# Load order, place of attention 1, norm chain of group 0 and g_norm load in a fused linear-attention and ELU-MLP kernel

## The chip, the cores and the metric

The kernel runs on one NeuronCore of a Trainium2 chip. The metric is the device time of the slowest core in microseconds; there is only one core here. Times below are medians of several runs, always compared with runs of the kernel before on the same chip, interleaved with them. A kernel's profile is one further look at one execution; its span is about 2 us shorter than the time of that same run (328.3 against 330.45 us for the kernel before).

Engines in the profile: PE is TensorE (matrix products), PEld its weight loads, DVE is VectorE, ACT is ScalarE, POOL is GpSimd, SP is SyncE, which here issues the loads and stores.

## The reference, cut to what matters

```python
# q, k, v: (8, 8, 576, 64) float32; g_norm: (64,)
kv  = einsum('bhsd,bhse->bhde', k, v)
out = einsum('bhsd,bhde->bhse', q, kv)
rms = sqrt(mean(out * out, -1) + 1e-6)
x   = (out / rms * g_norm)  ->  (4608, 512)          # 4608 tokens
h   = x @ w_in                                       # w_in  (512, 2048)
g   = where(h > 0, h, exp(min(h, 0)) - 1)            # ELU
y   = g @ w_out                                      # w_out (2048, 512)
```

The kernel works in nine groups of 512 tokens: one for each batch entry, and one for the 64 tokens that each entry has left. A group goes through attention, the first product (`mm1`, eight steps of 8 matmuls with the ELU behind each), and the second product (`mm2`, four row blocks of 16 matmuls).

## The kernel before

All compute is in program order on each engine; an engine that waits holds up everything behind it: in the profile before, TensorE is idle for 2.07 us ahead of 90.92 us, waiting for `xT` of group 2, and the second-product matmuls of group 1 that stand behind those products come at 94.58, though the DVE steps they read had ended by 90.20. These are the parts that matter.

```python
g_src = bass.AP(tensor=g_norm.tensor, offset=g_norm.offset, ap=[[1, 64], [1, 1]])
for i in range(2):
    nc.scalar.dma_start(out=g_col[i * 64 : i * 64 + 64, :], in_=g_src)   # 64 x 4 bytes, issued by ACT
...
def mm1(T, i, cols=..., relu=False):
    h_ps = ps_m1.tile([P, 2, G], FP32, tag="mm1")      # two such PSUM buffers in all
    ...                                                # 8 matmuls 128x512
    nc.scalar.activation(e, h_ps, AF.Exp)              # ACT
    ...                                                # relu=True: ACT also copies max(h, 0) out
    def rest():                                        # DVE: elu_e, then gT (reads h_ps if relu=False)
...
# group 0, norm: norm_a = square (ACT) + sum (DVE); norm_b = ln, exp (ACT) + scale (DVE)
norm_a(0); norm_a(1); norm_b(0); norm_a(2); turn(0); norm_b(1); norm_a(3)
turn(1); norm_b(2); turn(2); norm_b(3); turn(3)        # turn = 4 transposes (PE) + copy with g_col
...
at = attention(1)
for i in range(8):
    mm1(0, i, cols, relu=(i % 2 == 1))()
    if i == 5:
        at["q"]()
at["kv"]()
for s, n in enumerate(("se0", "se1", None, "x")):      # attention 1, covered by half of mm2(0)
    for j in range(2):
        mm2(0, j, 4 * s, 4 * s + 4)
    if n:
        at[n]()

at = attention(2)
steps = {1: "q", 2: "kv", 3: "se0", 5: "se1", 7: "x"}
for i in range(8):                                     # the loop of group 1
    rest = mm1(1, i)
    if i < 7:
        mm2(0, 2 + i // 4, 4 * (i % 4), 4 * (i % 4) + 4)
    rest()
    if i in steps:
        at[steps[i]]()
mm2(0, 3, 12, 16)
# then the loops of groups 2 to 8, all alike
```

`attention(T)` gives five steps: "q" transposes q (copied out by DVE, then ACT), "kv" forms the 64x64 products, "se0" and "se1" each apply them to half of the rows and normalize (square on ACT, sum on DVE, ln/exp on ACT, scale on DVE), "x" transposes the result into `xT`, which the next loop's `mm1` reads. All five share one PSUM tile, `at`.

TensorE's idle stretches in the start are partly filled with `idle(n)`, matmuls of zeros that nobody reads.

Of the kernel before, what the change touches and what calls it, by code (L numbers as in the profile page):

```python
# [8 lines left out]
FP32 = mybir.dt.float32  # L9
# [3 lines left out]
AX = mybir.AxisListType  # L13
# [3 lines left out]
def kernel(  # L17
# [43 lines left out]
    ctx.enter_context(tc.manual_schedule())  # L61

    g_col = const.tile([P, 1], FP32, name="g_col")
    g_src = bass.AP(tensor=g_norm.tensor, offset=g_norm.offset, ap=[[1, 64], [1, 1]])
    for i in range(2):
        nc.scalar.dma_start(out=g_col[i * 64 : i * 64 + 64, :], in_=g_src)
    eps_col = const.tile([P, 1], FP32, name="eps_col")
    nc.vector.memset(eps_col, 1e-6)
    bd_kv = const.tile([P, B, NPAIR, P], BF16, name="bd_kv")
# [41 lines left out]
    def fetch(b):  # L111
        fetch_q(b)
        for name, src in (("k", k), ("v", v)):
            out_, in_ = fetch_kv(name, src, b)
            nc.sync.dma_start(out=out_, in_=in_)

    def fetch_w_in(s):
        st = stage_tile()[:, 0:2048]
        nc.sync.dma_start(
            out=st.rearrange("p (c f) -> p c f", c=KC),  # L120
            in_=moe_w_in.rearrange("(c p) f -> p c f", p=P)[:, :, s * 512 : s * 512 + 512],
        )
        raw["wi", s] = st

    def fetch_w_out(s):
        st = stage_tile()[:, 0:2048]
        nc.sync.dma_start(
            out=st.rearrange("p (c f) -> p c f", c=KC),
            in_=moe_w_out.rearrange("(c p) f -> p c f", p=P)[:, 4 * s : 4 * s + 4, :],
        )  # L130
        raw["wo", s] = st
# [18 lines left out]
    def cast_q(b, eng):  # L150
        sv = q_tile(b)
        for j in range(J):
            copy_on(eng, bf["q", b][:, j], sv[:, j])

    def cast_kv(name, b, eng):
        sv = kv_tile(name, b)
        for lo, hi in ((0, 2), (2, 4), (4, 6), (6, 8), (8, 9)):
            copy_on(eng, bf[name, b][:, lo:hi], sv[:, lo:hi])

    def cast_w_in(s, eng):  # L160
        st = raw.pop(("wi", s)).rearrange("p (c f) -> p c f", c=KC)
        for c in range(KC):
            copy_on(eng, w_in_sb[:, c, s * 512 : s * 512 + 512], st[:, c, :])

    def cast_w_out(s, eng):
        st = raw.pop(("wo", s)).rearrange("p (c f) -> p c f", c=KC)
        for c in range(KC):
            copy_on(eng, w_out_sb[:, 4 * s + c, :], st[:, c, :])
# [50 lines left out]
                    )  # L219

    def square(se_ps, n):
        sq = attp.tile([P, 2, DM], BF16, name="sq", tag="sq")[:, 0:n, :]
        nc.scalar.activation(sq, se_ps, AF.Square)  # L223
        return sq

    def sum_heads(sq, n):
        ss = attp.tile([P, 2 * H], FP32, name="ss", tag="ss")[:, 0 : n * H]
        nc.vector.reduce_sum(  # L228
            out=ss, in_=sq.rearrange("p c (h e) -> p (c h) e", h=H), axis=AX.X
        )  # L230
        return ss

    def inv_rms(ss):
        nc.scalar.activation(ss, ss, AF.Ln, bias=eps_col, scale=1.0 / D)  # L234
        nc.scalar.activation(ss, ss, AF.Exp, scale=-0.5)  # L235

    def scale_rows(xs, se_ps, ss, n):
        nc.vector.tensor_tensor(  # L238
            out=xs.rearrange("p c (h e) -> p (c h) e", h=H),
            in0=se_ps.rearrange("p c (h e) -> p (c h) e", h=H),  # L240
            in1=ss.to_broadcast([P, n * H, D]),
            op=ALU.mult,
        )

    def attention(T):
        st = {}

        def kv():
            if T == B:
                return  # L250
            kv_ps = at_tile(FP32)
            for u in range(2):
                kv_mm(T, [kv_ps[:, 0:512], kv_ps[:, 512:1024]], u)
            kv_v = kv_ps.rearrange("p (s x e) -> p s x e", s=2, e=P)[:, :, 0:2, :]
            bd_v = bd_kv[:, T].rearrange("p (s u) e -> p s u e", s=2)
            for l in range(2):
                ls = slice(l * 64, l * 64 + 64)
                nc.scalar.copy(bd_v[ls, :, :, ls], kv_v[ls, :, :, ls])

        def q_t():  # L260
            qt_ps = at_tile(BF16).rearrange("p (r t) -> p r t", r=NPAIR)
            for p in range(NPAIR):
                q_t_mm(bf["q", T], qt_ps, p)
            qT = attp.tile([P, NPAIR, G], BF16, name="qT", tag="qT")
            st["qT"] = qT
            nc.vector.tensor_copy(out=qT[:, 0:2, :], in_=qt_ps[:, 0:2, :])  # L266
            nc.scalar.copy(qT[:, 2:4, :], qt_ps[:, 2:4, :])  # L267

        def se(h):
            def run():  # L270
                se_ps = at_tile(FP32).rearrange("p (c f) -> p c f", c=2)
                for c in range(2):
                    se_mm(T, 2 * h + c, st["qT"], se_ps[:, c, :])
                ss = sum_heads(square(se_ps, 2), 2)
                inv_rms(ss)
                if h == 0:
                    st["xs"] = attp.tile([P, J, DM], BF16, name="xs", tag="xs")
                scale_rows(st["xs"][:, 2 * h : 2 * h + 2, :], se_ps, ss, 2)

            return run  # L280

        def x_t():
            xs = st["xs"]
            xt_ps = at_tile(BF16).rearrange("p (r t) -> p r t", r=NPAIR)
            for c in range(KC):
                for j in range(J):
                    nc.tensor.transpose(  # L287
                        xt_ps[:, c, j * P : j * P + P],
                        xs[:, j, c * P : c * P + P],
                        ident,  # L290
                    )
            x = attp.tile([P, KC, G], BF16, name="xT", tag="xT")
            xT[T] = x
            nc.vector.tensor_scalar(  # L294
                out=x[:, 0:2, :], in0=xt_ps[:, 0:2, :], scalar1=g_col, scalar2=None, op0=ALU.mult
            )
            nc.scalar.mul(x[:, 2:4, :], xt_ps[:, 2:4, :], g_col)  # L297

        return {"kv": kv, "q": q_t, "se0": se(0), "se1": se(1), "x": x_t}
# [61 lines left out]
    def mm2_half(T, i):  # L361
        mm2(T, i // 2, 8 * (i % 2), 8 * (i % 2) + 8)
# [25 lines left out]
    for u in range(2):  # L388
        for out_, in_ in halves:
            nc.sync.dma_start(  # L390
                out=out_[:, 2 * u : 2 * u + 2, :], in_=in_[:, 2 * u : 2 * u + 2, :]
            )
    for s in range(3):
        fetch_w_in(s)

    q_st = q_tile(0)
# [5 lines left out]
    def idle(n):  # L402
        for _ in range(n):
            nc.tensor.matmul(idle_ps[:, 0, :], lhsT=ident, rhs=zeros, start=True, stop=True)  # L404
# [3 lines left out]
    for s in range(2):  # L408
# [2 lines left out]
        for p in (2 * s, 2 * s + 1):  # L411
            q_t_mm(bf["q", 0], qt_ps, p)
        idle(2)
    fetch_w_in(3)
    kv_st = [kv_tile(name, 0) for name in "kv"]
    kv_ps = [ps_m2.tile([P, DM], FP32, name="kv_ps", tag="mm2") for _ in range(2)]
    for u in range(2):
# [35 lines left out]
    one = [t.rearrange("p (c f) -> p c f", c=1) for t in se_ps]  # L453
    ss = {}

    def norm_a(j):
        ss[j] = sum_heads(square(one[j], 1), 1)

    def norm_b(j):
        inv_rms(ss[j])  # L460
        scale_rows(xs0[:, j : j + 1, :], one[j], ss[j], 1)

    def turn(j):
        js = slice(j * P, j * P + P)
        xt = xt_ps[:, j % 2, j // 2]
        for c in range(KC):
            nc.tensor.transpose(xt[:, c, :], xs0[:, j, c * P : c * P + P], ident)
        if j % 2 == 0:
            nc.scalar.mul(x0[:, :, js], xt, g_col)
        else:  # L470
            nc.vector.tensor_scalar(
                out=x0[:, :, js], in0=xt, scalar1=g_col, scalar2=None, op0=ALU.mult
            )
            idle(2)

    norm_a(0)
    norm_a(1)
    norm_b(0)
    norm_a(2)
    turn(0)  # L480
    norm_b(1)
    norm_a(3)
    turn(1)
    norm_b(2)
    turn(2)
    norm_b(3)
    turn(3)


    for s in range(4):  # L490
        cast_w_in(s, Q)
    fetch(1)
    cast_q(1, Q)
    cast_kv("k", 1, Q)
    cast_kv("v", 1, Q)
    for s in range(4):
        fetch_w_out(s)
    for s in range(4):
        cast_w_out(s, Q)

    def cast_all(b):
        cast_q(b, Q)
        if b < B:
            cast_kv("k", b, Q)
            cast_kv("v", b, Q)

    fetch(2)
    cast_all(2)
    at = attention(1)
    for i in range(8):  # L510
        cols = (slice(0, 256), slice(256, 512)) if i == 0 else (slice(0, 512),)
        mm1(0, i, cols, relu=(i % 2 == 1))()
        if i == 5:
            at["q"]()
    at["kv"]()
    for s, n in enumerate(("se0", "se1", None, "x")):
        for j in range(2):
            mm2(0, j, 4 * s, 4 * s + 4)
        if n:
            at[n]()  # L520

    at = attention(2)
    steps = {1: "q", 2: "kv", 3: "se0", 5: "se1", 7: "x"}
    fetch(3)
    for i in range(8):
        rest = mm1(1, i)
        if i < 7:
            mm2(0, 2 + i // 4, 4 * (i % 4), 4 * (i % 4) + 4)
        rest()
        if i in steps:  # L530
            at[steps[i]]()
    mm2(0, 3, 12, 16)

    steps = {0: "kv", 1: "q", 2: "se0", 4: "se1", 6: "x"}
    for T in range(2, NT):
# [45 lines left out]
```

## Time and profile before

| | before |
|---|---|
| median (4 runs of its first comparison) | 331.76 us (330.75 to 332.81) |
| first square of group 0 / first product of group 0 | 15.93 / 26.56 us |
| DVE's copy of `xT` of group 1 / of group 2 starts | 60.93 / 90.12 us |
| last unbroken run of second-product matmuls (71 of them) starts / span | 307.26 / 328.3 us |

The lines below are from the profile page of the kernel before: the busy time, and TensorE's busy tenths and granted clock in 40 equal slices of 8.2 us.

```profile
PE 299.2 (91%) x1903; PEld 151.0 (46%) x1939; DVE 180.3 (55%) x216; ACT 152.1 (46%) x216; POOL 78.5 (24%) x140
...
PE   8648796799789999999999999999999999999993
...
PEclk9996999999979999999999999999999999999999
```

TensorE is busy 91% of the span, and the slices that fall short lie in the first 98 us, but for the last one. The clock shows a dip to 0.6 in the fourth slice (from 24.6 us) and one to 0.7 in the twelfth (from 90.3 us).

The next view is busy time by stretch of the same run, with the granted clock, the DMA share (packet times over the time of 16 engines; it can come out a little above 1, here up to 1.07) and GB/s as the last three columns.

```profile
core 0: us, PE busy (x) PEld busy (x) DVE busy (x) ACT busy (x) POOL busy (x), PEclk, DMA share, GB/s
5.00:7.00 2.00, 2.00 (x8) 0.80 (x7) 0.43 (x1) 0.78 (x2) 0.00 (x0) 1.00 0.55 163
19.00:26.50 7.50, 2.68 (x16) 1.27 (x17) 3.88 (x7) 3.05 (x9) 5.71 (x11) 0.78 1.07 373
26.50:31.90 5.40, 5.30 (x25) 3.13 (x24) 0.68 (x1) 1.03 (x2) 4.01 (x8) 0.68 1.06 390
33.50:47.20 13.70, 11.53 (x64) 5.48 (x67) 8.18 (x11) 7.68 (x9) 13.70 (x22) 1.00 1.06 378
47.20:61.70 14.50, 10.39 (x100) 5.96 (x101) 8.89 (x9) 7.10 (x13) 8.38 (x16) 1.00 0.46 170
87.00:90.90 3.90, 1.85 (x20) 1.22 (x20) 3.65 (x5) 0.83 (x2) 0.00 (x0) 1.00 0.00 0
90.90:97.00 6.10, 5.53 (x34) 2.23 (x35) 1.02 (x2) 2.61 (x3) 0.00 (x0) 0.72 0.60 191
150.00:300.00 150.00, 149.05 (x938) 75.23 (x955) 90.26 (x104) 72.56 (x97) 18.13 (x32) 1.00 0.25 88
```

From 150 to 300 us TensorE is busy in 149.05 of 150 us: there it is the limit, and the change leaves that part alone. The time to win is earlier: 2.68 of 7.5 us busy in the norm of group 0, 11.53 of 13.7 in its first product, 10.39 of 14.5 where attention 1 stands alone, and 1.85 of 3.9 at the end of the loop of group 1. Three stretches have a low clock (0.78, 0.68 and 0.72).

The timeline of TensorE in the same run (start, duration, instruction group, and in brackets the idle time before it and what the profile says ended it):

```profile
26.56 5.29 PE L313 MATMUL h_ps<-xT,w_in_sb 128*128 128x256 bf16 x24
33.45 3.61 PE L313 MATMUL h_ps<-xT,w_in_sb 128*128 128x512 bf16 x15 [1.60 <-DVE gT L331]
38.54 3.61 PE L313 MATMUL h_ps<-xT,w_in_sb 128*128 128x512 bf16 x16 [1.47 <-POOL w_out_sb L137]
...
43.64 3.61 PE L313 MATMUL h_ps<-xT,w_in_sb 128*128 128x512 bf16 x15 [0.59 <-DVE gT L331]
...
90.92 0.59 PE L313 MATMUL h_ps<-xT,w_in_sb 128*128 128x512 bf16 x2 [2.07 <-DVE xT L294]
```

In the first product TensorE starts anew at 33.45, 38.54 and 43.64, that is every 5.1 us for two steps whose matmuls take 3.6 us: step i+2 needs the PSUM buffer that DVE's `gT` of step i still reads. The idle time at 38.54 is put down to a POOL cast of w_out, which that product doesn't read; what ended it is DVE's `gT`, which ended at 37.26 + 1.22 = 38.48 us. DVE's timeline in the same run:

```profile
37.26 1.22 DVE L331 TENSOR_TENSOR gT<-elu_e,h_ps 128x1024 bf16<-128x1024 bf16 x1
```

The first 24 products, 128x256 each, take 5.29 us, or 220 ns each. At 90.92 TensorE has been idle 2.07 us for `xT`.

### The profile page before, as it was taken

The numbers are of one execution on the slowest core, as the hardware profiler recorded it, in microseconds if no ns is written. First come the engines' busy times: TensorE is split into PE (matmuls) and PEld (weight loads), VectorE is DVE, ScalarE is ACT, GpSimd is POOL, SyncE is SP. The second block draws the span as 40 slices with busy tenths as digits, with TensorE's granted clock in tenths as the row PEclk, the third lists the DMA queues.
The fourth block names the chain that finished last, engine by engine and source line by source line (L and its number), as shares of the span: only waits on it lengthen the run. The fifth ranks groups of instructions, "written<-read, shape, count | busy, mean of one in ns | idle before, by whom it ended". The sixth has DMA issues, their size and how long they took to land.

```text
span 328.3 us, 4746 instructions
## 1 busy us (share of the span) xinstructions
PE 299.2 (91%) x1903; PEld 151.0 (46%) x1939; DVE 180.3 (55%) x216; ACT 152.1 (46%) x216; POOL 78.5 (24%) x140
## 2 busy tenths in 40 slices
PE   8648796799789999999999999999999999999993
PEld 3414353354335454545454554455445545444441
DVE  3462566367824774676467646755675577445400
ACT  3552574446345544555455445543654454433320
POOL 0077998063007200630070017001100000000000
PEclk9996999999979999999999999999999999999999
DMA  6999994670067106710851094114301010101122
GB/s 207 394 381 381 387 374 149 189 293 0 2 206 275 64 0 194 288 66 0 272 209 64 3 319 163 64 43 104 85 29 64 2 64 0 66 0 64 66 61 67
DMA packets 28565, 46.44 MB, mean 141 GB/s; under 512 B 5504, under 2 KB 13696, under 8 KB 28544
## 3 DMA queue, kind: packets, MB, share of 16 engines
q1 hardware_dynamic: 28384, 46.14, 39.8%
q8 instruction: 15, 0.25, 0.3%
q14 instruction: 6, 0.05, 0.0%
q10 hardware_dynamic: 160, 0.00, 0.0%
HBM read 36.70 MB, written 9.44 MB: 141 GB/s over the span
## 4 chain that ended last, share of the span: by engine, by line
PE 76%; DVE 7%; DMA 7%; ACT 4%; POOL 2%; issue 2%; SPq 1%; DVEq 0%
PE o_ps L347 34%; PE h_ps L313 33%; DMA st<-in_k_dram 4%; DMA st<-in_v_dram 3%; PE at L182 2%; DVE gT L331 2%; PE at L287 2%; PE at L204 2%; DVE ss L228 2%; DVE xs L238 2%; PE at L192 2%; POOL v_bf L137 1%; DVE elu_e L328 1%; ACT elu_e L321 1%; POOL k_bf L137 1%
## 5 line engine op out<-in xcount | busy, mean ns | idle before, releaser
L313 PE MATMUL h_ps<-xT,w_in_sb 128*128 128x512 bf16 (+1 forms) x565 | 136.3, 383 | 9.6 <-DVE xT L294 2.9
L347 PE MATMUL o_ps<-w_out_sb,gT 128*128 128x512 bf16 x561 | 134.4, 379 | 0.8
L321 ACT ACTIVATE elu_e<-h_ps 128x1024 bf16<-128x1024 f32 x72 | 73.4, 1021 | 57.0 <-PE h_ps L313 55.5
L313 PEld LDWEIGHTS <-w_in_sb 128*128 128x128 bf16 x584 | 56.5, 100 | 71.4 <-issue 10.3
L347 PEld LDWEIGHTS <-gT 128*128 128x128 bf16 x576 | 56.3, 98 | 67.5 <-issue 0.8
L331 DVE TENSOR_TENSOR gT<-elu_e,h_ps 128x1024 bf16<-128x1024 bf16 x68 | 83.0, 1221 | 7.1
L328 DVE TENSOR_SCALAR elu_e<-elu_e 128x1024 bf16<-128x1024 bf16 x72 | 34.0, 473 | 91.1 <-ACT elu_e L321 91.1
L137 POOL CAST q_bf<-st 128x512 bf16<-128x512 f32 x32 | 19.2, 637 | 131.8 <-DMA st<-in_q_dram 108.7
L357 ACT COPY o_sb<-o_ps 128x512 f32<-128x512 f32 x36 | 21.0, 583 | 21.8 <-PE o_ps L347 21.7
L238 DVE TENSOR_TENSOR xs<-at,ss 128x1024 bf16<-128x1024 f32 (+1 forms) x18 | 21.0, 1166 | 10.8 <-ACT ss L235 10.8
L228 DVE TENSOR_REDUCE ss<-sq 128x16 f32<-128x1024 bf16 (+1 forms) x20 | 22.2, 1112 | 8.2 <-ACT sq L223 8.0
L223 ACT ACTIVATE sq<-at 128x1024 bf16<-128x1024 f32 (+1 forms) x18 | 17.5, 977 | 17.0 <-PE at L204 14.4
L137 POOL CAST k_bf<-st 128x512 bf16<-128x512 f32 (+1 forms) x35 | 19.8, 608 | 6.6 <-DMA st<-in_k_dram 6.6
L137 POOL CAST v_bf<-st 128x512 bf16<-128x512 f32 (+1 forms) x35 | 19.2, 592 | 0.5
L297 ACT ACTIVATE xT<-at,g_col 128x1024 bf16<-128x1024 bf16 x8 | 8.9, 1114 | 20.0 <-DVE xT L294 20.0
L234 ACT ACTIVATE ss<-ss,eps_col 128x16 f32<-128x16 f32 (+1 forms) x20 | 6.1, 304 | 22.3 <-DVE ss L228 22.3
L404 PE MATMUL idle_ps<-zeros,ident 128*128 128x512 bf16 x41 | 13.1, 460 | 1.6 <-POOL ident masks.py:199 1.4
L267 ACT COPY qT<-at 128x1024 bf16<-128x1024 bf16 x8 | 8.1, 1012 | 11.4 <-DVE qT L266 11.4
L137 POOL CAST w_in_sb<-st 128x512 bf16<-128x512 f32 x16 | 9.1, 613 | 17.1 <-DMA st<-in_moe_w_in_dram 17.1
L182 PEld LDWEIGHTS <-k_bf 64*128 64x128 bf16 x288 | 8.2, 94 | 7.1 <-issue 3.9
L204 PE MATMUL at<-bd_kv,qT 128*128 128x128 bf16 x120 | 9.1, 219 | 2.5 <-DVE xs L238 2.5
L204 PEld LDWEIGHTS <-qT 128*128 128x128 bf16 x128 | 8.4, 98 | 6.4 <-issue 3.1
(44 smaller groups left out, 112.4 us busy)
## 6 DMA issues: line engine op xcount, KB each, us to landing
st<-in_q_dram SPq DMA_DIRECT2D x16, 512.0 KB, 5.7
out_dram<-o_sb SPq DMA_DIRECT2D x16, 512.0 KB, 2.7
st<-in_k_dram SPq DMA_DIRECT2D x7, 1152.0 KB, 8.8
st<-in_v_dram SPq DMA_DIRECT2D x7, 1152.0 KB, 11.2
st<-in_moe_w_in_dram SPq DMA_DIRECT2D x4, 1024.0 KB, 15.0
st<-in_moe_w_out_dram SPq DMA_DIRECT2D x4, 1024.0 KB, 14.4
st<-in_k_dram SPq DMA_DIRECT2D x2, 576.0 KB, 8.1
st<-in_v_dram SPq DMA_DIRECT2D x2, 576.0 KB, 9.0
```

The costliest lines, as they stand in the source:

```text
L137: eng.tensor_copy(out=out_, in_=in_)
L182: nc.tensor.matmul(kv_ps[s][:, u * P : u * P + P], lhsT=bf["k", T][rows, j, 2 * u : 2 * u + 2, :], rhs=bf["v", T][rows, j, 2 * u : 2 * u + ...
L204: nc.tensor.matmul(ov[:, u, :, s, :], lhsT=qT[:, p, j * P : j * P + P], rhs=bd_kv[:, T, p, :], start=True, stop=True,)
L223: nc.scalar.activation(sq, se_ps, AF.Square)
L228: nc.vector.reduce_sum(out=ss, in_=sq.rearrange("p c (h e) -> p (c h) e", h=H), axis=AX.X)
L238: nc.vector.tensor_tensor(out=xs.rearrange("p c (h e) -> p (c h) e", h=H), in0=se_ps.rearrange("p c (h e) -> p (c h) e", h=H), in1=ss.to_b ...
L313: nc.tensor.matmul(h_ps[:, a, cs], lhsT=w_in_sb[:, c, f * P : f * P + P], rhs=x[:, c, cs], start=(c == 0), stop=(c == KC - 1),)
L321: nc.scalar.activation(e, h_ps, AF.Exp)
L328: nc.vector.tensor_scalar(out=e, in0=e, scalar1=1.0, scalar2=1.0, op0=ALU.min, op1=ALU.subtract)
L331: nc.vector.tensor_tensor(out=gT[T][:, 2 * i : 2 * i + 2, :], in0=e, in1=h, op=ALU.add if relu else ALU.max,)
L347: nc.tensor.matmul(o_ps[T, j], lhsT=gT[T][:, f, j * P : j * P + P], rhs=w_out_sb[:, f, :], start=(f == 0), stop=(f == FC - 1),)
L357: nc.scalar.copy(o_sb[T][:, j % 2, :], o_ps.pop((T, j)))
```

## The change

The intent: load only half of w_in, then q/k/v of group 1, then the rest, so that attention 1 can run inside the first product of group 0 and fill its holes; and run the norm of group 0 with all squares first, one joint ln/exp for two rows, and the copies on ACT.

```diff
-    for i in range(2):
-        nc.scalar.dma_start(out=g_col[i * 64 : i * 64 + 64, :], in_=g_src)
 ...                                        # after the loads of q/k/v of group 0:
+    for i in range(2):
+        nc.sync.dma_start(out=g_col[i * 64 : i * 64 + 64, :], in_=g_src)
-    for s in range(3):
+    for s in range(2):
         fetch_w_in(s)
 ...                                        # norm of group 0
-    norm_a(0) ... turn(3)                  # as shown above; turn(1), turn(3) end with idle(2)
+    sq = [square(one[j], 1) for j in range(J)]   # four buffers for these squares
+    for j in range(3):
+        sums(j)
+    inv_rms(ss_all[:, 0 : 2 * H])
+    inv_rms(ss[2])
+    scale_rows(row 0); turn(0, A); idle(2)
+    scale_rows(row 1); turn(1, A); idle(2)
+    sums(3); inv_rms(ss[3])
+    scale_rows(row 2); turn(2, A); idle(2)
+    scale_rows(row 3); turn(3, V)
 ...                                        # loads and casts
-    for s in range(4):
-        cast_w_in(s, Q)
-    fetch(1); casts of q/k/v of group 1
-    w_out: four loads, then four casts
+    for s in range(2):
+        cast_w_in(s, Q)
+    fetch(1); cast_all(1)
+    w_in 2 and 3: loads, then casts
+    w_out: load and cast, four times
 ...                                        # group 0's first product
+    steps = {2: "q", 3: "kv", 4: "se0", 6: "se1"}
     for i in range(8):
         mm1(0, i, cols, relu=(i % 2 == 1))()
-        if i == 5:
-            at["q"]()
-    at["kv"](), then se0, se1, x among 32 matmuls of mm2(0)
+        if i in steps:
+            at[steps[i]]()
+    mm2_half(0, 0); mm2_half(0, 1)          # a half is 8 matmuls
+    at["x"]()
+    mm2_half(0, 2)
 ...                                        # loop of group 1
+    halves = {0: 3, 2: 4, 4: 5, 6: 6}
-        if i < 7:
-            mm2(0, 2 + i // 4, 4 * (i % 4), 4 * (i % 4) + 4)
+        if i in halves:
+            mm2_half(0, halves[i])
-    mm2(0, 3, 12, 16)
+    mm2_half(0, 7)
```

More of the change, by code (lines that the diff above doesn't have):

```diff
@@ L63 @@
     g_col = const.tile([P, 1], FP32, name="g_col")
-    g_src = bass.AP(tensor=g_norm.tensor, offset=g_norm.offset, ap=[[1, 64], [1, 1]])
-    for i in range(2):
-        nc.scalar.dma_start(out=g_col[i * 64 : i * 64 + 64, :], in_=g_src)
     eps_col = const.tile([P, 1], FP32, name="eps_col")
@@ L221, in square @@
     def square(se_ps, n):
-        sq = attp.tile([P, 2, DM], BF16, name="sq", tag="sq")[:, 0:n, :]
+        sq = attp.tile([P, n, DM], BF16, name="sq", tag=f"sq{n}", bufs=2 if n == 2 else 4)
         nc.scalar.activation(sq, se_ps, AF.Square)
@@ L392 @@
             )
-    for s in range(3):
+    g_src = bass.AP(tensor=g_norm.tensor, offset=g_norm.offset, ap=[[1, 64], [1, 1]])
+    for i in range(2):
+        nc.sync.dma_start(out=g_col[i * 64 : i * 64 + 64, :], in_=g_src)
+    for s in range(2):
         fetch_w_in(s)
@@ L413 @@
         idle(2)
-    fetch_w_in(3)
     kv_st = [kv_tile(name, 0) for name in "kv"]
@@ L454, with turn @@
     ss = {}
-    def norm_a(j):
-        ss[j] = sum_heads(square(one[j], 1), 1)
-    def norm_b(j):
-        inv_rms(ss[j])
-        scale_rows(xs0[:, j : j + 1, :], one[j], ss[j], 1)
-    def turn(j):
+    def turn(j, eng):
         js = slice(j * P, j * P + P)
@@ L467, in turn @@
             nc.tensor.transpose(xt[:, c, :], xs0[:, j, c * P : c * P + P], ident)
-        if j % 2 == 0:
+        if eng is A:
             nc.scalar.mul(x0[:, :, js], xt, g_col)
@@ L473, in turn, with sums @@
             )
-            idle(2)
-    norm_a(0)
-    norm_a(1)
-    norm_b(0)
-    norm_a(2)
-    turn(0)
-    norm_b(1)
-    norm_a(3)
-    turn(1)
-    norm_b(2)
-    turn(2)
-    norm_b(3)
-    turn(3)
-    for s in range(4):
-        cast_w_in(s, Q)
-    fetch(1)
-    cast_q(1, Q)
-    cast_kv("k", 1, Q)
-    cast_kv("v", 1, Q)
-    for s in range(4):
-        fetch_w_out(s)
-    for s in range(4):
-        cast_w_out(s, Q)
+    ss_all = attp.tile([P, J * H], FP32, name="ss_all", tag="ss_all", bufs=1)
+    ss = [ss_all[:, j * H : j * H + H] for j in range(J)]
+    sq = [square(one[j], 1) for j in range(J)]
+    def sums(j):
+        nc.vector.reduce_sum(
+            out=ss[j], in_=sq[j].rearrange("p c (h e) -> p (c h) e", h=H), axis=AX.X
+        )
+    for j in range(3):
+        sums(j)
+    inv_rms(ss_all[:, 0 : 2 * H])
+    inv_rms(ss[2])
+    scale_rows(xs0[:, 0:1, :], one[0], ss[0], 1)
+    turn(0, A)
+    idle(2)
+    scale_rows(xs0[:, 1:2, :], one[1], ss[1], 1)
+    turn(1, A)
+    idle(2)
+    sums(3)
+    inv_rms(ss[3])
+    scale_rows(xs0[:, 2:3, :], one[2], ss[2], 1)
+    turn(2, A)
+    idle(2)
+    scale_rows(xs0[:, 3:4, :], one[3], ss[3], 1)
+    turn(3, V)
     def cast_all(b):
@@ L505, in cast_all @@
             cast_kv("v", b, Q)
+    for s in range(2):
+        cast_w_in(s, Q)
+    fetch(1)
+    cast_all(1)
+    for s in range(2, 4):
+        fetch_w_in(s)
+    for s in range(2, 4):
+        cast_w_in(s, Q)
+    for s in range(4):
+        fetch_w_out(s)
+        cast_w_out(s, Q)
     fetch(2)
-    cast_all(2)
     at = attention(1)
+    steps = {2: "q", 3: "kv", 4: "se0", 6: "se1"}
     for i in range(8):
@@ L512 @@
         mm1(0, i, cols, relu=(i % 2 == 1))()
-        if i == 5:
-            at["q"]()
-    at["kv"]()
-    for s, n in enumerate(("se0", "se1", None, "x")):
-        for j in range(2):
-            mm2(0, j, 4 * s, 4 * s + 4)
-        if n:
-            at[n]()
+        if i in steps:
+            at[steps[i]]()
+    mm2_half(0, 0)
+    mm2_half(0, 1)
+    at["x"]()
+    mm2_half(0, 2)
+    cast_all(2)
+    fetch(3)
     at = attention(2)
+    halves = {0: 3, 2: 4, 4: 5, 6: 6}
     steps = {1: "q", 2: "kv", 3: "se0", 5: "se1", 7: "x"}
-    fetch(3)
     for i in range(8):
         rest = mm1(1, i)
-        if i < 7:
-            mm2(0, 2 + i // 4, 4 * (i % 4), 4 * (i % 4) + 4)
+        if i in halves:
+            mm2_half(0, halves[i])
         rest()
```

## The prediction

> **What bounds it now.** From 97 us on, TensorE is the limit: busy time by stretch is 12.8 of 13.0 us (97 to 110) and 149.1 of 150 us (150 to 300). The change leaves that part alone, so only the first 92 us can shrink. There TensorE does 2.7 of 7.5 us (19 to 26.5), 11.5 of 13.7 (33.5 to 47.2), 10.4 of 14.5 (47.2 to 61.7), 1.9 of 3.9 (87 to 90.9). Loads keep the DMA engines full until about 48 us, but the timeline's waits show DVE and ACT latency, not data, holding TensorE:
> - Group 0's norm: the last transpose starts at 25.04, the first product at 26.56. The granted clock is 0.68 from 26.5 to 31.9; a 128x256 product takes 220 ns there.
> - First product of group 0: product i+2 waits for `gT` of i (same PSUM buffer): 1.9 + exp 1.02 + `elu_e` 0.75 + `gT` 1.22, about 5.1 us a pair for 3.5 us of TensorE.
> - Attention 1 after it: square 1.03, sum 1.22, ln/exp 0.53, scale 1.23, twice, with only 32 second-product matmuls (6.9 us) as cover.
>
> **What the change does.** The same bytes are loaded; q/k/v of group 1 go before w_in 2 and 3. From landings in the trace (1 MB about 2.8 us) I estimate k/v of group 1 cast by 31 us, w_in 2 and 3 by 33.5 and 36, w_out by 47.5, each before its use. The g_norm load moves to SP, off the path.
>
> Step 1, norm: all four squares (0.54 each) run first, one ln/exp serves rows 0 and 1, three copies go to ACT, the last idle matmuls go. Replaying by hand with traced durations, scale 0 starts at 18.7 (was 17.85), but the last transpose at 22.7 and products at 23.1: gain 3.4 us. [...] it should keep full clock: 1.7 us more. [...]
>
> Step 2, attention 1 inside the first product: the replay gives 32.5 us from first product to the loop of group 1, against 35.9 before (34.2 at full clock): that loop starts at 55.6 instead of 62.45. New TensorE holes: about 2.4 us before kv of group 1 (`qT` copies), 2.75 us where half 1 of the second product waits for the last `gT`. One half (1.73 us) more is left for the next loop.
>
> Step 3, loop of group 1: bound by the DVE chain. Replaying before gives its waits within 0.4 us; after, it is 0.9 us longer (30.1), absorbing the extra half. Its final hole shrinks, which may avoid the low clock at 91 to 97 us (0.72, about 1.5 us).
>
> Sum: 6.85 - 0.9 = 5.9 us, plus up to 1.5 at 91, less about 0.9 for a possible new low-clock spell: some 6.5 us. All is on the critical path: the TensorE-bound part simply starts earlier.
>
> **Time.** 324.8 us, 321.8 to 328.5; faster by over 2% 0.47, within 2% 0.52, slower 0.01.
>
> **What would show it.** First product at 23 us, clock near 1.0; qT and kv between products of group 0; loop of group 1 starting at 55 to 56; group 2's products at 85 to 86; then the same density. POOL should not be what TensorE waits for.
>
> **What would make it wrong.** TensorE slow in the new holes (1.7 us each); ACT's in-order blocking (exp 3 behind the ACT half of `qT`, exp 5 and 7 behind ln/exp) worse than replayed; w_in or w_out cast late because POOL casts slow down beside DVE (0.57 to 0.73 us each now); g_col landing after 19.9 us.

Two passages are cut from step 1: the reason given for full clock, and the source it named; no trace of this case shows them. That TensorE keeps full clock there was the author's estimate. The sum came to some 6.5 us, and the 1.7 us of full clock are contained in its 6.85 (62.45 - 55.6 us), as 35.9 against 34.2.

Some numbers to the text, from the two profiles. The DMA share before is 0.87 from 0 to 20 us and 1.06 from 20 to 50 us. POOL's casts of 128x512 before took 0.61 us each from 28.2 to 30.5 us, while DVE did nothing, and 0.61 to 1.07 us from 37.4 to 48 us, with DVE busy in 6.45 of 10.6 us. In-order blocking of ACT: after the change, exp 3 started at 33.61 us, behind the ACT half of `qT` (32.70 + 1.01), though its products had ended at 31.57 (29.68 + 1.89). The 1.7 us for a slow hole is an estimate; half of a spell of 3.41 us at a granted clock of 0.50 is as much, and the spell of a_again at 33.6 us made `xT` 1 0.8 us later.

## The result, and the profile after

The changed kernel takes 322.52 us (median of 4 runs, 322.06 to 323.25) against 331.76 us. The ratio is 0.9723, with a 95% interval of 0.9684 to 0.9762: faster by 2.8%. Ratios here are the mean time of one kernel's fast runs over that of the other's of the same rounds, so not quite the ratio of the medians that are quoted. Run again later on another occasion it took 323.13 us, ratio 0.9753 (label a_again below).

The profile page of the changed kernel, the same lines as above:

```profile
PE 295.8 (92%) x1905; PEld 149.7 (47%) x1941; DVE 179.2 (56%) x215; ACT 151.8 (47%) x215; POOL 78.4 (24%) x140
...
PE   8777686988899999999999999999999999999993
...
PEclk9999999999999999999999999999999999999999
```

The clock is at 0.9 or more in every slice. Busy time by stretch (the columns are as before; the stretches follow this kernel's own stages):

```profile
5.00:7.00 2.00, 2.00 (x7) 0.73 (x6) 0.47 (x2) 0.85 (x2) 0.00 (x0) 1.00 1.07 373
11.00:13.00 2.00, 1.64 (x13) 0.73 (x13) 1.32 (x4) 1.26 (x5) 0.00 (x0) 1.00 0.67 223
15.00:22.00 7.00, 5.20 (x39) 2.53 (x38) 5.04 (x8) 5.44 (x13) 4.58 (x8) 1.00 1.07 377
22.00:26.50 4.50, 3.66 (x28) 2.37 (x26) 1.85 (x3) 1.82 (x2) 2.74 (x5) 1.00 1.06 392
26.50:54.50 28.00, 19.78 (x153) 10.61 (x156) 17.76 (x21) 15.34 (x22) 26.04 (x43) 1.00 1.06 381
54.50:84.00 29.50, 26.70 (x187) 13.86 (x188) 19.19 (x22) 13.91 (x20) 10.59 (x19) 1.00 0.29 106
84.00:97.00 13.00, 11.96 (x96) 6.30 (x98) 4.23 (x6) 6.82 (x9) 3.19 (x6) 1.00 0.81 282
140.00:290.00 150.00, 149.05 (x938) 75.09 (x955) 90.30 (x104) 73.66 (x99) 18.19 (x32) 1.00 0.26 88
```

From 5 to 7 us the loads run at 373 GB/s instead of 163; there is a slow spot of 223 GB/s from 11 to 13 us in its place. The norm (15 to 22 us) has TensorE busy in 5.20 of 7 us, and the clock is 1.00 everywhere. The steady part is unchanged: 149.05 of 150 us.

TensorE's timeline in the changed kernel:

```profile
22.03 3.64 PE L310 MATMUL h_ps<-xT,w_in_sb 128*128 128x256 bf16 x24
...
33.86 1.18 PE L179 MATMUL at<-v_bf,k_bf 64*128 64x128 bf16 x36 [2.28 <-POOL w_in_sb L134]
...
51.51 0.60 PE L344 MATMUL o_ps<-w_out_sb,gT 128*128 128x512 bf16 x2 [2.84 <-DVE gT L328]
...
54.57 1.89 PE L310 MATMUL h_ps<-xT,w_in_sb 128*128 128x512 bf16 x8
```

The first product starts at 22.03 us, and 24 products of 128x256 take 3.64 us. Attention 1's kv comes at 33.86, inside the first product; the profile blames a POOL cast of w_in for the 2.28 us before it, but kv doesn't read w_in. It needs the tile `at`, which ACT's copy of `qT` leaves at 33.71 (32.70 + 1.01). ACT's timeline in the same run:

```profile
32.70 1.01 ACT L264 COPY qT<-at 128x1024 bf16<-128x1024 bf16 x1 [2.69 <-DVE qT L263]
```

At 51.51 there is the largest new hole, 2.84 us for the last `gT`. The loop of group 1 starts at 54.57.

Set side by side, the two profiles divide the gain in this way:

| stage | before | after | gain |
|---|---|---|---|
| start to first square | 15.93 | 15.02 | 0.91 |
| first square to first product | 10.63 | 7.01 | 3.62 |
| first product to `xT` of group 1 (DVE) | 34.37 | 31.02 | 3.35 |
| `xT` of group 1 to `xT` of group 2 | 29.19 | 30.53 | -1.34 |
| `xT` of group 2 to last run of second-product matmuls | 217.14 | 215.79 | 1.35 |
| last run to end | 21.04 | 21.03 | 0.0 |
| sum | 328.3 | 320.4 | 7.9 |

The experiments ask which edit owns which of these rows.

### The profile page after: what moved, and what is told of

The parts are those of the page before. It is cut to its first block, busy times and chain, and to the rows that moved or that the text cites. A ratio compares the mean times of both kernels' runs of the same rounds, so it can differ in the third digit from the quotient of the medians.

```text
span 320.4 us, 4746 instructions
## 1 busy us (share of the span) xinstructions
PE 295.8 (92%) x1905; PEld 149.7 (47%) x1941; DVE 179.2 (56%) x215; ACT 151.8 (47%) x215; POOL 78.4 (24%) x140
## 3 DMA queue, kind: packets, MB, share of 16 engines
q1 hardware_dynamic: 28544, 46.14, 41.1%
## 4 chain that ended last, share of the span: by engine, by line
PE 78%; DMA 7%; DVE 5%; ACT 5%; issue 2%; SPq 1%; POOL 0%; DVEq 0%
PE o_ps L344 36%; PE h_ps L310 33%; DMA st<-in_moe_w_in_dram 5%; DMA st<-in_v_dram 3%; ACT elu_e L318 2%; PE at L179 2%; PE at L284 2%; DVE gT L328 2%; PE at L189 2%; PE at L201 2%; DVE ss L225 1%; DVE elu_e L325 1%; ACT sq L220 1%; DVE xs L235 1%; ACT elu_h L322 1%
## 5 line engine op out<-in xcount | busy, mean ns | idle before, releaser
L310 PE MATMUL h_ps<-xT,w_in_sb 128*128 128x512 bf16 (+1 forms) x564 | 133.8, 376 | 6.3 <-DVE gT L328 3.6
L310 PEld LDWEIGHTS <-w_in_sb 128*128 128x128 bf16 x584 | 55.2, 98 | 65.2 <-issue 3.2
L325 DVE TENSOR_SCALAR elu_e<-elu_e 128x1024 bf16<-128x1024 bf16 x72 | 33.3, 462 | 87.8 <-ACT elu_e L318 87.8
L235 DVE TENSOR_TENSOR xs<-at,ss 128x1024 bf16<-128x1024 f32 x16 | 19.6, 1225 | 9.9 <-ACT ss L232 9.9
L225 DVE TENSOR_REDUCE ss<-sq 128x16 f32<-128x1024 bf16 x16 | 19.5, 1218 | 4.8 <-ACT sq L220 4.7
L231 ACT ACTIVATE ss<-ss,eps_col 128x16 f32<-128x16 f32 x16 | 4.9, 307 | 24.7 <-DVE ss L225 24.7
L134 POOL CAST w_in_sb<-st 128x512 bf16<-128x512 f32 x16 | 9.8, 655 | 15.8 <-DMA st<-in_moe_w_in_dram 15.8
L179 PE MATMUL at<-v_bf,k_bf 64*128 64x128 bf16 x252 | 8.3, 216 | 3.0 <-POOL w_in_sb L134 2.3
```

Source lines behind the costliest of these rows:

```text
L134: eng.tensor_copy(out=out_, in_=in_)
L179: nc.tensor.matmul(kv_ps[s][:, u * P : u * P + P], lhsT=bf["k", T][rows, j, 2 * u : 2 * u + 2, :], rhs=bf["v", T][rows, j, 2 * u : 2 * u + ...
L225: nc.vector.reduce_sum(out=ss, in_=sq.rearrange("p c (h e) -> p (c h) e", h=H), axis=AX.X)
L235: nc.vector.tensor_tensor(out=xs.rearrange("p c (h e) -> p (c h) e", h=H), in0=se_ps.rearrange("p c (h e) -> p (c h) e", h=H), in1=ss.to_b ...
L310: nc.tensor.matmul(h_ps[:, a, cs], lhsT=w_in_sb[:, c, f * P : f * P + P], rhs=x[:, c, cs], start=(c == 0), stop=(c == KC - 1),)
L325: nc.vector.tensor_scalar(out=e, in0=e, scalar1=1.0, scalar2=1.0, op0=ALU.min, op1=ALU.subtract)
```

## The experiments

The milestones of all profiles, in us from the start of the span, to be read along with the texts below ("low clock" lists when the trace's clock records start a spell at half clock, up to 100 us, and its length; the granted clock in the spells is 0.50, as from 23.16 to 29.99 us in before):

| label | first square | first product | `xT` 1 | `xT` 2 | span | low clock |
|---|---|---|---|---|---|---|
| before | 15.93 | 26.56 | 60.93 | 90.12 | 328.3 | 23.2 (6.8), 91.4 (3.4) |
| e1_gnorm | 14.61 | 25.25 | 60.09 | 89.56 | 327.7 | 22.5 (6.8), 53.2 (3.4), 90.8 (3.4) |
| e2_norm | 16.35 | 23.36 | 56.17 | 85.75 | 324.3 | 50.9 (3.4), 88.4 (3.4) |
| e3_attn | 16.63 | 27.28 | 60.92 | 91.09 | 327.9 | 24.0 (6.8), 41.1 (3.4) |
| e4_warm | 16.42 | 26.43 | 58.91 | 88.24 | 326.3 | 89.2 (3.4) |
| e5_glate | 16.17 | 29.61 | 62.49 | 91.73 | 329.8 | 10.9 (3.4), 21.1 (10.2), 92.8 (3.4) |
| e7_newload | 17.41 | 28.26 | 61.08 | 90.48 | 327.3 | 12.5 (3.4), 22.8 (6.8) |
| e11_gnorm_norm | 14.95 | 21.96 | 54.13 | 83.58 | 321.8 | 84.9 (3.4) |
| after | 15.02 | 22.03 | 53.05 | 83.58 | 320.4 | none |
| a_again | 14.92 | 21.93 | 53.84 | 84.19 | 321.0 | 33.6 (3.4) |
| e10_noidle | 14.72 | 21.73 | 55.43 | 85.59 | 322.4 | 21.8 (3.4), 35.5 (3.4) |
| e6_oldload | 15.26 | 22.27 | 57.98 | 88.14 | 325.0 | 37.7 (3.4) |
| e8_xearly | 15.32 | 22.32 | 52.12 | 83.00 | 319.9 | 34.4 (3.4) |
| e9_fours | 15.39 | 22.40 | 51.92 | 81.04 | 317.9 | 34.5 (3.4) |

All outputs are right. One run of the kernel before took 462.05 us beside the second set, and one of e3_attn took 333.81 us, over 1.5% above the fastest of its six; both count as slow and are left out of the ratios.

### The parts, one at a time

**e1_gnorm**: the kernel before with only the g_norm load moved.

```diff
-        nc.scalar.dma_start(out=g_col[...], in_=g_src)      # first thing on ACT
+        nc.sync.dma_start(out=g_col[...], in_=g_src)        # SP, behind q/k/v of group 0
```

> The kernel before with one edit: the two g_norm loads are issued by SP behind q/k/v of group 0 instead of by ACT at the start. My theory, formed after the two traces (before, 4 to 8 us: 248 to 278 GB/s at a DMA share of 0.78; after: 368 to 391): the 4-byte g_norm packets on a second queue slow the first loads by 0.9 us, so the first square starts at 15.0 us instead of 15.9, and the whole is 0.9 us faster (331.8 to about 330.9). Rival, what the prediction assumed: that load is off the path, 0 us, and the 0.9 us is chance.

Measured: 329.57 us against 331.99, ratio 0.993 (0.9898 to 0.9963). The first square came at 14.61 us. Busy time by stretch of this run, 5 to 7 and 11 to 13 us:

```profile
5.00:7.00 2.00, 2.00 (x12) 0.92 (x11) 0.43 (x1) 0.80 (x2) 0.00 (x0) 1.00 1.07 378
11.00:13.00 2.00, 1.59 (x19) 0.79 (x20) 1.37 (x4) 1.48 (x4) 0.00 (x0) 1.00 0.64 195
```

The drop in throughput follows the g_norm load: 378 GB/s where before there were 163, and 195 later, when nothing urgent is being loaded. The load is two DMAs of 64 elements of 4 bytes. The cast of the last part of v on ACT follows; its lines in the timelines of the kernel before and, second, of this run:

```profile
13.40 0.62 ACT L135 CAST v_bf<-st 128x512 bf16<-128x512 f32 x1
12.21 0.61 ACT L132 CAST v_bf<-st 128x512 bf16<-128x512 f32 x1
```

By these starts the effect is steadier than by one profile: in the five kernels that issue g_norm from ACT at the start, ACT's cast of the last part of v starts at 13.40, 13.82, 13.89, 13.91 and 14.10 us; in the nine others at 12.18 to 13.09, median 12.62. That is 1.27 us at the medians, and the profile of before (13.40) happened to be the earliest of its kind. So my rival, which was the prediction's own assumption that this load is off the path, falls. The median moved by 2.4 us; the interval allows 1.2 to 3.4, and the 1.3 us lie inside it. The granted clock of these runs was also a little higher on average, 0.979 against 0.973, so a part of the 2.4 us may be clock; that is not separated here.

**e2_norm**: the kernel before with only the new norm chain.

```diff
-    norm_a(0) ... turn(3)
+    sq = [...]; sums; joint inv_rms; ...; turn(3, V)         # as in the change
```

> The kernel before with only the norm chain of group 0 reordered (four squares first, joint ln/exp, three copies on ACT, idle matmuls after rows 0 to 2). My theory: from first square to first product 7.0 us instead of 10.6 (3.6 us), and the clock stays at 1.0 from 19 to 32 us (1.7 us more): about 5.3 us faster. Rival A, only the order counts and the clock spell comes anyway: 3.6 us. Rival B, what is won here is lost again because the first product then waits for w_in slice 2 or 3 or for q/k/v of group 1 in the old load order: under 3 us.

Measured: 326.31 us, ratio 0.9826 (0.9794 to 0.9857): 5.7 us. First square to first product took 7.01 us instead of 10.63, and no low-clock spell fell between 19 and 32 us. Nothing was lost behind it: first product to `xT` 1 took 32.81 us against 34.37, although this profile shows a new spell at 50.9. Rivals A and B fall.

**e3_attn**: the changed kernel with the old norm and the old g_norm load, so that only load order and attention move are new.

```diff
 # against the changed kernel
-    sq = [...]; sums; joint inv_rms; ...; turn(3, V)
+    norm_a(0) ... turn(3)
-    nc.sync.dma_start(out=g_col...)
+    nc.scalar.dma_start(out=g_col...)
```

> The changed kernel with the norm chain and the g_norm load of before: only the load order and the place of attention 1 are new. My theory: first product at 26.5 us as before, clock low there (0.68); first product to the loop of group 1 about 34.2 us at the low clock against 35.9 (1.7 us faster), that loop 1.3 us longer, low-clock spell at 91 to 97 gone (1.4 us): about 1.8 us faster in all. If instead the attention move is what makes most of the gain, as the change's wording suggests, it is 5 us or more faster.

Measured: 330.12 us over the five fast runs (330.74 with the slow one), ratio 0.9953 (0.9916 to 0.9991): 1.9 us by the medians, 1.6 by the ratio, close to the 1.8 expected. The part of the change that its title names first is worth the least. The three parts, 2.4, 5.7 and 1.9 us, add up to 10.0 us; the whole change gave 9.2.

### The clock by itself

**e4_warm**: the kernel before, the same chain, only more idle matmuls between its rows.

```diff
-            idle(2)                         # after rows 1 and 3
+        idle(2 if j == 3 else 4)            # after every row j
```

> The kernel before with only more idle matmuls in the norm of group 0 (4 after rows 0, 1, 2 instead of 2 after row 1; row 3 keeps 2), same order of the chain. It measures the clock spell by itself. My theory: clock 1.0 from 19 to 32 us, first product at about 26 us, 24 products of 128x256 in 3.6 us instead of 5.3: 1.7 us faster, up to 2.2 with the shorter last idles. Rival: the spell doesn't depend on the density there, or the first product phase is bound by DVE and ACT so that the slow clock costs nothing: 0 us.

Measured: 329.88 us, ratio 0.9945 (0.9892 to 0.9998), 2.1 us at the medians; the interval is wide because the six runs fall into two groups. Three had a granted clock of 0.992 to 0.999 and took 326.93 to 328.44 us; three had 0.977 or 0.978, like the kernel before (0.967 to 0.983), and took 331.31 to 331.80 us. So the added idle matmuls kept the clock up in about half of the runs. The profiled run is one of the first group. TensorE's timeline in it:

```profile
26.43 3.63 PE L313 MATMUL h_ps<-xT,w_in_sb 128*128 128x256 bf16 x23
```

The products took 3.63 us instead of 5.29 (one of the 24 records is missing) at nearly the same place, and first product to `xT` 1 fell from 34.37 to 32.48 us. So the low clock did cost time, although the first product is held up by DVE and ACT afterwards; the two groups of runs, on average 3.8 us apart, say the same.

**e10_noidle**: the changed kernel without its six idle matmuls.

```diff
     turn(0, A)
-    idle(2)
 ...                                        # the same after rows 1 and 2
```

> The changed kernel without the six idle matmuls between its transposed rows. If those keep the clock up (my reading of e4_warm), the low-clock spell at 23 to 30 us comes back and the time is about 1.7 us longer than the changed kernel's 323. Rival: the shorter chain alone[...]: same clock and time as the changed kernel.

Measured: 325.82 us, ratio 0.9855 (0.9807 to 0.9903), against 0.9753 for the changed kernel in its second set and 0.9723 in its first: 1.0 to 1.3 points slower, more than the 1.7 us expected. Two of its four runs had a granted clock of 0.989 (324.59 and 324.66 us), two of 0.974 and 0.975 (327.58 and 326.98 us); the profile is of the first and already has two spells, at 21.8 and 35.5 us. TensorE's timeline in this run:

```profile
20.34 0.38 PE L459 MATMUL xt_ps<-ident,xs 128*128 128x128 bf16 x4 [0.78 <-ACT xT L461]
21.50 0.40 PE L459 MATMUL xt_ps<-ident,xs 128*128 128x128 bf16 x4 [0.78 <-ACT xT L461]
21.73 5.30 PE L310 MATMUL h_ps<-xT,w_in_sb 128*128 128x256 bf16 x24
```

The products start as early as in the changed kernel (21.73) but take 5.30 us, although no gap between the rows was longer than 0.78 us. The short chain alone doesn't keep the clock; with the idle matmuls in it, none of the seven profiles (e2, e11, after, a_again, e6, e8, e9) has a spell between 19 and 32 us.

What precedes a spell can be read from the clock records. The spells' lengths are 3.41 us or two or three times that, and their starts fit a grid of 3.41 us (23.16 and 91.43 us in before are 20 steps apart) whose place differs from run to run (22.50 us, not 23.16, in e1_gnorm). I looked at TensorE's busy share in the grid stretch just ahead of each spell, in all 14 profiles up to 110 us. Each of the 22 stretches that a spell followed had a share of 0.25 to 0.42. Of the others at full clock two, of the changed kernel, had 0.41 and 0.42, and all the rest 0.45 or more; none was followed by a spell. So between 0.41 and 0.42 the share alone does not decide. Below, busy time by stretch for the two stretches of the kernel before that a spell followed:

```profile
19.75:23.16 3.41, 1.23 (x10) 0.56 (x10) 2.37 (x4) 1.26 (x6) 2.09 (x5) 1.00 1.04 385
88.02:91.43 3.41, 1.34 (x6) 0.48 (x5) 2.74 (x4) 0.53 (x1) 0.00 (x0) 1.00 0.00 0
```

1.23 and 1.34 of 3.41 us, or 0.36 and 0.39; and yet TensorE was never idle for longer than 2.07 us at a time in them. For e10_noidle the stretch is this one, with 0.32:

```profile
18.39:21.80 3.41, 1.08 (x14) 0.91 (x14) 2.04 (x4) 2.46 (x5) 1.45 (x4) 1.00 1.07 360
```

And two stretches of the changed kernel that no spell followed:

```profile
47.24:50.65 3.41, 1.43 (x7) 0.46 (x5) 2.26 (x4) 2.35 (x4) 2.96 (x6) 1.00 1.05 390
81.36:84.77 3.41, 2.47 (x17) 1.17 (x15) 2.67 (x4) 0.93 (x2) 0.00 (x0) 1.00 0.00 0
```

The first, which holds most of the 2.84 us hole, has 0.42, as much as one that a spell followed (e5_glate, 7.5 to 10.9 us). The second is the end of the loop of group 1, with 0.72.

The slow stretches differ in the same way. Their shares were 0.23 to 0.62 where another slow one followed (0.43, 0.62 and 0.47 in the first slow stretch of before, e1_gnorm and e3_attn) and 0.82 to 1.00 where the clock came back (1.00 in e10_noidle, 21.8 to 25.2 us, a spell of 3.41 us).

### Load order and attention move

**e7_newload**: the kernel before with only the load order new.

```diff
-    for s in range(4): cast_w_in(s, Q)
-    fetch(1); casts of q/k/v of group 1
+    for s in range(2): cast_w_in(s, Q)
+    fetch(1); casts of q/k/v of group 1
+    w_in 2 and 3: loads, then casts         # then w_out: load and cast, four times
```

> The kernel before with only the new load order (q/k/v of group 1 ahead of w_in 2 and 3; attention 1 stays after the first product). My theory: the order by itself is worth nothing: w_in 2 and 3 are cast at about 33.5 and 36 us, before products 4 and 6 want them at 38.5 and 43.6: within 0.5 us of before. Rival: the order helps by itself (DMA or POOL runs smoother): 1 us or more faster; or it hurts, because products 4 to 7 wait for w_in.

Measured: 330.67 us against 331.18, ratio 0.9993 (0.9957 to 1.003): nothing, as expected. Its first square is late (17.41) because a low-clock spell fell at 12.5 us, behind a stretch with a share of 0.25.

**e6_oldload**: the changed kernel with the old load order.

```diff
-    for s in range(2): fetch_w_in(s)
+    for s in range(3): fetch_w_in(s)        # the fourth a little later, as before
-    for s in range(2): cast_w_in(s, Q)
-    fetch(1); cast_all(1); w_in 2 and 3
+    for s in range(4): cast_w_in(s, Q)
+    fetch(1); cast_all(1)                   # then w_out: four loads, then four casts
```

> The changed kernel with the old load order (all of w_in before q/k/v of group 1). My theory: the order is what makes the move of attention 1 possible. q of group 1 is then cast at about 30.5 and v at about 37.4 us instead of 25.4 and 32.1, after TensorE wants them (28.8 and 33.9): the loop of group 1 starts about 3.5 us later, 325.5 to 326 us. Rival: the DVE and ACT chains hide the later cast, under 1 us.

Measured: 329.22 us, ratio 0.9926 (0.9889 to 0.9964), where the changed kernel on the same chip had 323.13: 6.1 us slower. Lines of this run's timeline:

```profile
29.33 0.23 PE L189 MATMUL at<-ident,q_bf 128*128 128x128 bf16 x1 [0.36 <-POOL q_bf L134]
...
35.28 0.29 PE L179 MATMUL at<-v_bf,k_bf 64*128 64x128 bf16 x4 [1.47 <-POOL v_bf L134]
```

TensorE waits for the casts of q and then of v of group 1, piece by piece (two of these waits are shown), and, as program order has it, all products behind them wait too: `xT` 1 comes at 57.98 instead of 53.84. That is 4.1 us, near the expected 3.5. The profiled run was the fastest of its six (327.17), so the profile doesn't account for the remaining 2 us. The granted clock of that run was 0.994, of the other five 0.975 to 0.984, so they had more time at half clock; where, no profile shows. The order that is worth nothing alone is what the move of attention 1 depends on: without it the whole (ratio 0.9926) is slower than with attention left where it was (e11 below, 0.9799).

**e11_gnorm_norm**: the changed kernel without the load order and the attention move.

```diff
 # against the kernel before: e1_gnorm and e2_norm together
```

> The kernel before with the g_norm load moved and the norm chain reordered, old load order and old place of attention 1: the changed kernel without its attention move. If the parts add up, e1_gnorm's 2.4 and e2_norm's 5.7 give 8.1 us, about 323.9 us, and the attention move with its load order is worth about 1 us on top (323.1). If it is worth what the prediction gave it (32.5 us from first product to the loop of group 1 against 34.2 at full clock, less 0.9: 0.8 us, and 1.5 us of clock), this run is 2.3 us slower than the changed kernel. If the attention move needs an early first product to pay, 3 us or more.

Measured: 324.50 us against 331.18, ratio 0.9799 (0.977 to 0.9828), where the changed kernel has 0.9753 and 0.9723. The two edits together give 6.7 us here, somewhat less than the 8.1 of their sum (the interval allows 5.7 to 7.6). So the attention move adds 0.5 to 0.8 points, about 1.5 to 2.5 us; its interval overlaps that of the changed kernel's second set (0.9722 to 0.9783), not that of the first (0.9684 to 0.9762). The milestones say how: first product to `xT` 1 takes 32.17 us here and 31.02 in the changed kernel, and `xT` 1 to `xT` 2 takes 29.45 here and 30.53 there, so that both reach `xT` 2 at 83.58 us. What the move wins in the first product, the loop of group 1 gives back. It has one half of the second product more to do, 32 instead of 28 matmuls of it ahead of its transposes, and in blocks of eight; which of the two costs the time no run isolates. In e9_fours below, with 28 again and in fours, it takes 29.12 us. The difference that is left comes after, and it is the clock. Busy time by stretch in this run, for two stretches of the grid:

```profile
81.44:84.85 3.41, 1.34 (x7) 0.48 (x5) 2.78 (x4) 0.49 (x1) 0.00 (x0) 1.00 0.00 0
84.85:88.26 3.41, 2.85 (x8) 0.99 (x7) 0.00 (x0) 1.10 (x2) 0.00 (x0) 0.50 0.47 150
```

And TensorE's timeline at the end of the first:

```profile
84.38 0.59 PE L310 MATMUL h_ps<-xT,w_in_sb 128*128 128x512 bf16 x2 [2.07 <-DVE xT L291]
```

Here TensorE waits for `xT` with four matmuls to do, the share is 0.39, and the next 3.41 us run at half clock. The changed kernel keeps eight matmuls for that place, and its share is 0.72. Both kernels had reached `xT` 2 at 83.58 us, and their spans differ by 1.4 us (321.8 and 320.4). The other profiles agree: from `xT` 2 to `xT` of group 3 it takes 29.88 or 29.89 us in the eight profiles without a spell there and 31.07 to 31.58 us in the six with one. Those six all keep four matmuls for that place; the one profile that keeps four and escaped, e7_newload, had a share of 0.47 in the stretch ahead.

### The cause behind the g_norm load

**e5_glate**: the kernel before with g_norm still issued by ACT, but late.

```diff
-        nc.scalar.dma_start(out=g_col[...], in_=g_src)      # at the start
+        nc.scalar.dma_start(out=g_col[...], in_=g_src)      # behind the k/v casts of group 0
```

> The kernel before with the two g_norm loads still issued by ACT, but after its casts of k and v of group 0 (about 14 us) instead of at the start. If the collision with the first loads of q/k/v is the cause, this gains what e1_gnorm gained (first square about 1.3 us earlier, 2 us in the median) though the queue is the old one. If the second queue itself is the cause, the loss comes with it and only moves to w_in: then also no delay of the first square; so only the first square at 15.9 us or later would say that the collision is not the cause. If g_col comes after 19 us, the copies of row 0 wait for it and some of the gain is lost.

Measured: 331.50 us against 331.18, ratio 1.0006 (0.9975 to 1.0038): no gain, and the test, the time of the first square, was badly chosen. The collision itself is gone: from 3 to 7 us the loads ran at 377 to 382 GB/s, and ACT's cast of the last part of v started at 12.18 us as in e1. But two new costs took its place. ACT spends 1.18 us issuing the two DMAs just ahead of the first square, and g_col then lands after 6.3 us. ACT's timeline in this run:

```profile
21.86 0.69 ACT L469 ACTIVATE xT<-xt_ps,g_col 128x512 bf16<-128x512 bf16 x1 [3.32 <-DMA g_col<-in_g_norm_dram]
```

The copy of row 0 waited 3.32 us for it. A low-clock spell at 10.9 us came on top. What this run shows is that the timing of the load, not the queue it is on, decides about k and v; and that, issued at 14.9 us by ACT, the load comes too late for row 0. Why 128 elements of 4 bytes hold up the other loads so much in the first 7 us, and hardly at all in this run (361 to 403 GB/s in each microsecond from 15 to 21), stays open.

### Two versions that go further

**a_again**: the changed kernel as it is, as the mate of the two below.

> The changed kernel again, on the same chip as the next three, so that they can be compared with it: 322.5 us (ratio to before 0.972), clock 1.0 from 19 to 97 us, loop of group 1 starting at 54.5 us. If the clock there differs from run to run, a median up to 2 us higher.

Measured: 323.13 us against 331.81 (332.13 with the slow run of 462.05), ratio 0.9753 (0.9722 to 0.9783). Its profile has one spell that the first one hadn't, at 33.6 us, behind a stretch with a share of 0.40 (the hole ahead of kv). It made `xT` 1 0.8 us later.

**e8_xearly**: the transposes of attention 1 no longer stand behind the last `gT` of the first product, and product 7 has no copy of max(h, 0) by ACT.

```diff
-        mm1(0, i, cols, relu=(i % 2 == 1))()
+        rest = mm1(0, i, cols, relu=(i % 2 == 1 and i < 7))
+        if i < 7:
+            rest()
-    mm2_half(0, 0); mm2_half(0, 1)
+    mm2(0, 0, 0, 14)
     at["x"]()
+    rest()
 ...
+        if i == 0:
+            mm2(0, 0, 14, 16)               # in the loop of group 1
```

> The changed kernel with the transposes of attention 1 moved ahead of the last gT of the first product (the last two matmuls of half 1 go into the next loop; product 7 without its relu copy). The hole of 2.84 us there (51.5 us, waiting for gT) is on the critical path by my theory: transposes at 49.6 instead of 51.95, loop of group 1 starts at about 52.4 instead of 54.5: 1.5 to 2.1 us faster than the changed kernel, about 320.7 us. Rival: the loop of group 1 is bound by DVE, which does the same work, so nothing is won: 322.5 us.

Measured: 321.03 us, ratio 0.9692 (0.9659 to 0.9725): 2.1 us faster than the changed kernel beside it. `xT` 1 starts at 52.12 against 53.84. TensorE's timeline in this run:

```profile
51.03 1.05 PE L284 MATMUL at<-ident,xs 128*128 128x128 bf16 x16 [0.98 <-DVE xs L235]
```

The wait ahead of the transposes is 0.98 us, where the hole was 2.84. The hole was on the critical path.

**e9_fours**: the same, and in the loop of group 1 the second product goes in fours behind each product, as in the kernel before, with the last 14 matmuls behind the transposes.

```diff
-        if i in halves:
-            mm2_half(0, halves[i])
+        # i = 0: two of block 0, two of block 1; i = 1..6: the next four each
-    mm2_half(0, 7)
+    mm2(0, 3, 2, 16)
```

> As e8_xearly, and the second product of group 0 in the loop of group 1 spread in fours after each product as in the kernel before, with the last 14 matmuls behind the transposes. My theory: that loop takes 29.2 us as before instead of 30.5, and its final hole is covered: 1.0 to 1.3 us faster than e8_xearly, about 319.5 us. Rival: the coarser spreading has no part in the 1.3 us longer loop, the same as e8_xearly.

Measured: 319.89 us, ratio 0.9652 (0.9611 to 0.9692), 1.1 us faster than e8_xearly and 3.2 us faster than the changed kernel. The intervals of e8 and e9 overlap, so the profile has to carry the step between them: `xT` 1 to `xT` 2 takes 29.12 us here and 30.88 in e8_xearly. TensorE's timeline:

```profile
78.75 3.18 PE L344 MATMUL o_ps<-w_out_sb,gT 128*128 128x512 bf16 x14
81.84 0.59 PE L310 MATMUL h_ps<-xT,w_in_sb 128*128 128x512 bf16 x2
```

The 14 matmuls fill the wait for `xT` entirely: no idle time is left ahead of the products at 81.84. This version beats both kernels.

## Why the prediction was right, point by point

The prediction gave 324.8 us, 321.8 to 328.5; measured were 322.5 and, again, 323.1. The time was inside the range. The chance of "faster by over 2%" had been put at 0.47, a little below that of "within 2%". The mechanism was right in the main and the gain was put too small: 6.5 us by its sum, 7.0 by its middle time, instead of 9.2.

- *TensorE is the limit from 97 us on, and what starts earlier ends earlier.* Right: 149.05 of 150 us busy in both, and last run to end 21.04 and 21.03 us.
- *Step 1, norm: gain 3.4 us.* It gained 3.62 us in the profile. *Full clock: 1.7 us more.* Right in size, shown by e4_warm (32.48 against 34.37 us, first product to `xT` 1), but no run bears out the reason, so this term came out by luck. Short gaps alone did not keep the clock up: in e10_noidle they are 0.78 us at most and the 24 products still take 5.30 us. With the idle matmuls behind rows 0 to 2, which the prediction did not count on, they take 3.64 us in the changed kernel.
- *Step 2: 32.5 us from first product to the loop of group 1.* 32.54 us (22.03 to 54.57). The two holes were foretold as 2.4 and 2.75 us and measured 2.28 and 2.84.
- *Step 3: that loop 0.9 us longer.* 1.34 us longer, from `xT` to `xT`. Replaying the in-order queues by hand with traced durations was worth the effort: its stage lengths were within half a microsecond.
- *Up to 1.5 us at 91 us for a low-clock spell that may not come.* 1.35 us in the profile, and e11_gnorm_norm shows the spell where fewer matmuls are kept for the wait.
- *About 0.9 us for a possible new spell.* The first profile of the changed kernel had none; a_again had one, which made `xT` 1 0.8 us later. The granted clocks say that this is common: 1.0 in the profiled run without a spell, 0.994 in a_again's, and 0.984 to 0.994 in six of the ten timed runs. As an average the allowance was about right (an estimate from these clocks).
- *"The g_norm load moves to SP, off the path."* This is the term that was mis-sized: it was put at 0 us. It is worth 0.9 us between the two profiles and 1.27 us by the starts of the cast of v in all of them. The line that would have told, 163 GB/s from 5 to 7 us with loads still queued, was in the profile of before; I had read the DMA share only in slices of 8 us.
- *POOL should not be what TensorE waits for.* Held, once the label at 33.86 is checked against what the instruction reads.

With 1.27 us instead of 0 for the load and none taken off for a new spell, the sum is 8.7 us. The profiles differ by 7.9 us and the medians by 9.2, because the profiled run of before, 330.45 us, was 1.3 us faster than the median of its kernel (its cast of the last part of v started 0.5 us earlier than the median of its kind).

## What to carry to other kernels

When an in-order start-up phase is rearranged, split the gain by edit before believing its title: here a 512-byte load moved out of the way of the first loads and a reordered norm with a handful of idle matmuls made about 7 of the 9 us, and the large restructuring about two. Filling holes early can merely move the loss to a later stage: here the loop of group 1 lost 1.1 us of what the first product had won, and got it back when its filler was spread in fours and kept for its last wait. Sparse stretches also cost clock here: behind 3.41 us with a TensorE busy share of 0.25 to 0.42, 22 spells of 3.41 to 10.2 us at half clock followed in the 14 profiles. A load order that is worth nothing by itself (ratio 0.9993) may still be the condition for another edit (6.1 us lost without it).
